# Second-layer operands moved to small buffers of their own, and the folded weights made in another buffer, in an attention-plus-FFN kernel

## The chip, the cores and the metric

The kernel runs on 1 core of a Trainium2 chip. The metric is the device time of one execution in microseconds (us). TensorE (PE) multiplies, VectorE (DVE) and ScalarE (ACT) do the elementwise work, SyncE (SP) issues the loads and GpSimd (POOL) the stores. Each engine works off its own list of instructions in order and waits on semaphores, so an instruction that waits holds up all that stands behind it in its list.

## The reference

For each of 4 batches (N = 6080 tokens, C = 256 channels) a channel attention, then a feed-forward network over all 24320 tokens:

```python
qn = q / (norm(q, axis=1) + 1e-06);  kn = k / (norm(k, axis=1) + 1e-06)
s = kn.transpose(0, 2, 1) @ qn / tau           # 256 x 256 for each batch
a = softmax(s)
x = (v @ a).reshape(24320, 256)
h = x @ w_in                                   # 256 -> 2048
return relu(h)**2 @ w_out                      # 2048 -> 256
```

## The kernel before

**The work.** The attention matrix of a batch is multiplied into w_in once (`fold7`), so that each token needs two products, 256 to 2048 and 2048 to 256. A float32 product is made as three of the shorter type fp32r: high by high, low by high, high by low; every operand therefore exists as a high part (an ACT or DVE cast) and a low part (a DVE subtraction). The first layer is a Winograd product of 2x2 blocks with 7 products instead of 8 (`m1` to `m7`, L600, three matmuls each), the second takes 8 units of three matmuls in each slot (`layer2`, L722).

**Chunks and slots.** The tokens run in 24 chunks, 6 for each batch; a chunk has T = 512 columns (the last of a batch 480) of two tokens each and 8 slots j of some 10 us, so a batch has 48 slots. In the slots j = 2 and 3 (`paired`, L581) the second layer of both slots together is a product of block pairs: `pair_unit` (L758, the operands K12 and KS4) and `pair_product` (L800, K11, KS2, KS3, K22, KS1), 42 matmuls instead of 48. Where T is below 512, each `pair_product` but K22's ends with a small matmul of 32 columns (L805) that closes the bank. The first and the last chunk are not paired.

**Operands.** First-layer operands of a slot (`wt`, 896 KB, 3 buffers) are loaded from the scratch `wsc` by `load_wt` (L527), second-layer operands (`wo`, 512 KB, 3 buffers) from `wosc` by `load_wo` (L182), those of the pair from `wss` by `load_ws` (L187), one or two at a time. They all go through SP's queue, in one order. Tile `th` (1 buffer) holds the split factors of the pair (`pair_split`, L786 and L787).

**Batch edges.** While a batch runs, the scores of the next are gathered; at slot 30 of the batch its attention matrix is made. Then, in slots 33 to 50, `fold7` makes the folded weights (PE L466, ACT L475 and L479), and `combine` (`combine_parts`, L500) turns them into first-layer operands: three casts on ACT (L518), three subtractions on DVE (L519) and a write to `wsc` from POOL (L521), one set in each of slots 40 to 43 and 47 to 50, built in a `wt` buffer. These stretches, some 100 us long, are called batch edges 1 to 3 here (about 500 to 650, 1040 to 1170 and 1560 to 1690 us).

**What sets the order.** The calls are written out by a table: `at(u, fn, ...)` puts a step at position u, counted in slots, and the engines' lists follow from that with a scheduler's choice in between. `TB`, `WB`, `OB` are numbers of buffers.

Of the kernel before, what the change touches and what calls it, by code (L numbers as in the profile page):

```python
# [16 lines left out]
P = 128  # L17
# [3 lines left out]
def tile_channel_attention_relu2_ffn(ctx, tc, kq, vT, tau, w_in, w_out, outT):  # L21
# [57 lines left out]
    SG = 1  # L79
    NP = 7  # L80
    K12, KS4, K11, KS2, KS3, K22, KS1 = range(NP)
    OB = 3
    wo = {}
    ws = {}
    wosc = {}
# [59 lines left out]
    def decode_w_out(g):  # L145
        W = work.tile([P, 4, C], F32, name="sq", tag="sq")
        decode_f64(raws.pop(("out", g)), W)
        halves = W.rearrange("p (f j) (e c) -> p j f e c", f=2, e=NH)
        for i in range(2):
            j = 2 * g + i  # L150
            w = wo[0, j] = work.tile([P, 2, 2, NH, P], F32R, name="wo", tag="wo", bufs=OB)
            nc.scalar.copy(out=w[:, 0], in_=halves[:, i])
            nc.vector.tensor_sub(out=w[:, 1], in0=halves[:, i], in1=w[:, 0])
            wosc[j] = scratch.tile([P, 2, 2, NH, P], F32, name=f"wosc{j}")
            nc.gpsimd.dma_start(out=wosc[j], in_=w.bitcast(F32))
            if g == SG:
                for k, f, e in ((K12, 1, 0), (K11, 0, 0), (K22, 1, 1)):
                    nc.gpsimd.dma_start(out=wss[:, k, i], in_=w[:, :, f, e].bitcast(F32))
        if g == SG:
            win["out"] = W  # L160

    def combine_w_out():

        W = win.pop("out").rearrange("p (f j) (e c) -> p f e j c", f=2, e=NH)
        a11, a12, a21, a22 = W[:, 0, 0], W[:, 1, 0], W[:, 0, 1], W[:, 1, 1]
        S = work.tile([P, 4, 2, P], F32, name="sq", tag="sq")
        s4, s2, s3, s1 = (S[:, i] for i in range(4))
        nc.vector.tensor_add(out=s1, in0=a21, in1=a22)
        nc.vector.tensor_sub(out=s2, in0=s1, in1=a11)
        nc.vector.tensor_sub(out=s3, in0=a11, in1=a21)  # L170
        nc.vector.tensor_sub(out=s4, in0=a12, in1=s2)
        for i, ks in enumerate(((KS4, KS2), (KS3, KS1))):
            x = S[:, 2 * i:2 * i + 2]
            w = work.tile([P, 2, 2, 2, P], F32R, name="wo", tag="wo", bufs=OB)
            nc.scalar.copy(out=w[:, :, :, 0], in_=x)
            nc.vector.tensor_sub(out=w[:, :, :, 1], in0=x, in1=w[:, :, :, 0])
            for k, half in zip(ks, range(2)):
                nc.gpsimd.dma_start(out=wss[:, k], in_=w[:, half].bitcast(F32))

    def load_wo(ci, j):  # L180
        w = wo[ci, j] = work.tile([P, 2, 2, NH, P], F32R, name="wo", tag="wo", bufs=OB)
        nc.sync.dma_start(out=w.bitcast(F32), in_=wosc[j])  # L182

    def load_ws(ci, k):
        n = min(2, NP - k)
        w = work.tile([P, 2, 2, 2, P], F32R, name="wo", tag="wo", bufs=OB)
        nc.sync.dma_start(out=w[:, :n].bitcast(F32), in_=wss[:, k:k + n])  # L187
        for i in range(n):
            ws[ci, k + i] = w[:, i]

# [310 lines left out]
    def combine_parts(b, g):  # L501

        eng = nc.vector
        u = us.pop((b, g))
        S = work.tile([P, 4, GW], F32, name="sq", tag="sq")
        s2, s3, s1, s4 = (S[:, i] for i in range(4))
        eng.tensor_add(out=s1, in0=u[:, 0, 1], in1=u[:, 1, 1])
        eng.tensor_sub(out=s2, in0=s1, in1=u[:, 0, 0])
        eng.tensor_sub(out=s3, in0=u[:, 0, 0], in1=u[:, 0, 1])
        eng.tensor_sub(out=s4, in0=u[:, 1, 0], in1=s2)  # L510
        for i in range(2):
            j = 2 * g + i
            if i and b:
                yield
            w = work.tile([P, 2, NP, P], F32R, name="wt", bufs=WB)
            js = slice(i * P, (i + 1) * P)
            for o, x in ((w[:, :, 0:2], u[:, :, 0, js]), (w[:, :, 2:3], u[:, 1:2, 1, js]), (w[:, :, 3:7], S[:, :, js])):
                nc.scalar.copy(out=o[:, 0], in_=x)  # L518
                eng.tensor_sub(out=o[:, 1], in0=x, in1=o[:, 0])  # L519
            wsc[b, j] = scratch.tile([P, 2, NP, P], F32, name=f"wsc{j}", bufs=2)  # L520
            nc.gpsimd.dma_start(out=wsc[b, j], in_=w.bitcast(F32))  # L521
            if b == 0:
                wt[0, j] = w
# [55 lines left out]
    raw2 = {}  # L579

    def paired(q):  # L581
        return 0 < q[0] < len(chunks) - 1 and q[1] // 2 == SG

    marks = {"ACT": [], "DVE": []}
    LEAD = 0.9
# [112 lines left out]
    def layer2(q, c, e):  # L698
# [12 lines left out]
        w = T // 2  # L711
        if tail and (c, e) == ("11", 0):
            ends["sum"] = work.tile([P, HMAX], F32, name="tt", tag="tt", bufs=TB)
            nc.scalar.copy(out=ends["sum"][:, :w], in_=outs[1, 1][:, w:T])
        spans = [(o, 0, T, first, last or final and j == NJ - 2 and (c, e) == ("12", 1))]
        if tail and n and e:
            if c == "22":
# [190 lines left out]
    def at(u, fn, *args):  # L908
        side.setdefault(round(u, 3), []).append((fn, args))
# [25 lines left out]
    for b in range(1, B):  # L935
        u0 = (b - 1) * QB
        first, last = (NJ + 2 if b == 1 else 0), 30
        for i in range(NT // 2):
            u, k = u0 + first + i * (last - first) // (NT // 2), 2 * i
            if k % G == 0:  # L940
                at(u - 3.4, score_load, b, k // G)
            at(u - 0.8, score_norm, b, k)
            if b > 1 or k > LATE[-1]:
                at(u - 1.0, score_split, b, k)
                at(u - 0.5, score_split, b, k + 1)
                at(u + MID, score_burst, b, [k, k + 1])
        end = u0 + last
        at(end - 0.6, squares_split, b)
        at(end + MID, norms_wide, b)
        at(end + 1.6, lambda b=b: exps(b, s_acc[b]))  # L950
        at(end + 2 + MID, attnT, b)
        for g in range(0, NG, 2):
            u = end + 3 + 3.5 * g
            if b == 1:
                at(u - 3.5, load_wins2, g)
            for i in range(NP):
                at(u + i - (0.7 if b == 1 else 2.5), right7, b, g, i)
                at(u + i + MID, fold7, b, g, i)
            for i in range(2):
                at(u + NP + 2 * i, combine, b, g + i)  # L960
                at(u + NP + 2 * i + 1, combine, b, g + i)
    for n, (ci, j) in enumerate(quads):
        if ci:
            at(n - 1.5, load_wt, ci, j)
            if not paired((ci, j)):
                at(n - 0.3, load_wo, ci, j)
            elif j % 2 == 0:
                for k, u in ((K12, -0.3), (K11, 0.3), (KS3, 3.75), (KS1, 5.0)):
                    at(n + u, load_ws, ci, k)
                for u, fn in ((2.2, right3), (2.6, right1), (2.8, right2), (3.4, right4)):  # L970
                    at(n + u, fn, ci)
                for u, k in ((3.1, KS2), (3.9, KS3), (4.85, K22), (5.3, KS1)):
                    at(n + u, pair_split, ci, k)
                for u, k in ((2.6, K11), (3.6, KS2), (4.6, KS3), (5.13, K22), (5.6, KS1)):
                    at(n + u, pair_product, ci, k)
# [84 lines left out]
```

## Time and profile before

| | us |
|---|---|
| median of 3 runs | 2135.79 |
| the three runs | 2134.65, 2135.79, 2140.91 |
| profiled execution, its own time | 2138.98 |
| its span in the profile | 2137.1 |
| PE busy | 2126.3 (99%) |
| DVE busy | 1816.0 (85%) |
| ACT busy | 1456.2 (68%) |
| POOL busy | 90.3 (4%) |

PE is busy for all but 10.8 us of the span, and its granted clock is 1.00 in every stretch. A matmul's busy time includes a modelled end that overlaps with the next one, so what a matmul costs is read from start to start of the rows of a timeline.

### The profile page before, as it was taken

To read this page: it belongs to the slowest core of one execution; us is meant where nothing else is said; L and a number is where in the kernel's file an instruction comes from. 1 tells how busy PE (TensorE), PEld (TensorE's weight loads), DVE (VectorE), ACT (ScalarE), POOL (GpSimd) and SP (SyncE) were. 2 spreads that over 40 slices of the span, in tenths; PEclk is the share of its full clock that TensorE was granted. 3 is DMA by queue.
4 is the path that set the end of the run, shared out by engine and by line. 5 is a ranking of instruction groups with operands and counts; after the bars stand their busy time and mean duration, and the time that the engine had idled before them with its cause. 6 is when DMAs were issued, how large, how long until landed. Compare 5 with 4: busy or idle time off the path is not lost.

```text
span 2137.1 us, 27056 instructions
## 1 busy us (share of the span) xinstructions
PE 2126.3 (99%) x9756; PEld 1775.4 (83%) x9756; DVE 1816.0 (85%) x2549; ACT 1456.2 (68%) x2411; POOL 90.3 (4%) x167
## 2 busy tenths in 40 slices
PE   9999999999999999999999999999999999999999
PEld 8888888888888888888888888888888888888888
DVE  7898999989999889898899988989789778778765
ACT  6787777766776767666667676767666656656654
POOL 0120000011000000000000000000000000000000
PEclk9999999999999999999999999999999999999999
DMA  9777755467785564456768555456576655555542
GB/s 362 296 285 271 248 188 193 165 245 256 254 309 202 187 227 158 174 195 219 270 222 303 204 189 207 156 176 224 198 269 225 233 180 185 177 180 182 179 170 83
DMA packets 101557, 461.83 MB, mean 216 GB/s; under 512 B 11824, under 2 KB 14512, under 8 KB 94640
## 3 DMA queue, kind: packets, MB, share of 16 engines
q1 hardware_dynamic: 85152, 391.23, 52.7%
q0 software_dynamic: 16128, 68.76, 8.1%
q8 instruction: 77, 1.26, 0.2%
q14 instruction: 56, 0.46, 0.1%
q10 hardware_dynamic: 144, 0.12, 0.0%
HBM read 390.33 MB, written 69.73 MB: 215 GB/s over the span
## 4 chain that ended last, share of the span: by engine, by line
issue 49%; PE 47%; POOL 2%; DMA 1%; ACT 1%; DVE 1%; POOLq 0%; ACTq 0%; SPq 0%
PE o L722 18%; PE h L600 11%; PE z L600 6%; PE x L600 3%; PE x L800 2%; PE x L240 2%; PE o L758 1%; POOL outT L743 1%; PE h L240 1%; PE o L240 1%; DMA wsc<-wt 1%; PE o L800 1%; PE h L420 0%; DMA kqt<-kq 0%; POOL wsc L521 0%
## 5 line engine op out<-in xcount | busy, mean ns | idle before, releaser
L722 PE MATMUL o<-g,wo 128*128 128x512 f32 (+1 forms) x3552 | 903.5, 388 | 0.7 <-DMA wo<-wosc 0.7
L722 PEld LDWEIGHTS o<-g,wo 128*128 128x128 f32 x3552 | 664.5, 188 | 135.4 <-DVE g L631 1.8
L600 PE MATMUL h<-vt,wt 128*128 128x512 f32 (+1 forms) x2304 | 616.3, 388 | 2.0 <-DMA wt<-wsc 1.6
L600 PEld LDWEIGHTS h<-vt,wt 128*128 128x128 f32 x2304 | 431.4, 188 | 93.0 <-ACT x L642 2.7
L600 PE MATMUL z<-vt,wt 128*128 128x512 f32 (+1 forms) x1152 | 325.4, 390 | 1.7 <-ACT z L651 1.4
L600 PEld LDWEIGHTS z<-vt,wt 128*128 128x128 f32 x1152 | 210.4, 188 | 45.0 <-ACT z L651 4.6
L620 DVE TENSOR_TENSOR g<-r,g 128x512 fp32r<-128x512 f32 (+1 forms) x296 | 201.7, 682 | 48.9 <-ACT g L619 46.7
L630 ACT CAST g<-s 128x1024 fp32r<-128x1024 f32 (+1 forms) x148 | 153.9, 1040 | 114.9 <-DVE s L629 114.7
L631 DVE TENSOR_TENSOR g<-s,g 128x1024 fp32r<-128x1024 f32 (+1 forms) x148 | 179.2, 1211 | 51.5 <-ACT g L630 50.6
L615 ACT ACTIVATE r<-z 128x512 f32<-128x512 f32 (+1 forms) x148 | 87.7, 592 | 176.2 <-PE z L600 168.7
L616 ACT ACTIVATE r<-r 128x512 f32<-128x512 f32 (+1 forms) x296 | 186.4, 630 | 5.8
L629 DVE SCALAR_TENSOR_TENSOR s<-s 128x1024 f32<-128x1024 f32 (+1 forms) x148 | 178.9, 1209 | 1.0
L600 PE MATMUL x<-vt,wt 128*128 128x512 f32 (+1 forms) x576 | 161.0, 387 | 0.0
L786 ACT CAST th<-pair 128x1024 fp32r<-128x1024 f32 (+1 forms) x88 | 92.1, 1046 | 91.8 <-PE x L800 77.2
L651 ACT COPY z<-h 128x512 f32<-128x512 f32 (+1 forms) x192 | 110.5, 575 | 33.8 <-PE h L600 33.6
L220 DVE TENSOR_TENSOR acc<-acc,sq 128x1024 f32<-128x1024 f32 x92 | 112.5, 1223 | 22.9 <-ACT sq L219 20.6
L600 PEld LDWEIGHTS x<-vt,wt 128*128 128x128 f32 x576 | 108.1, 188 | 21.6
L642 ACT COPY x<-h 128x512 f32<-128x512 f32 (+1 forms) x192 | 110.9, 578 | 4.1 <-PE h L600 3.7
L664 ACT COPY m<-h 128x512 f32<-128x512 f32 (+1 forms) x192 | 110.9, 578 | 1.0
L787 DVE TENSOR_TENSOR th<-pair,th 128x1024 fp32r<-128x1024 f32 (+1 forms) x88 | 106.5, 1210 | 1.9 <-ACT th L786 1.7
L572 DVE TENSOR_TENSOR vt<-v,vt 128x512 fp32r<-128x512 f32 (+1 forms) x144 | 95.9, 680 | 13.3 <-ACT vt L571 13.0
L669 DVE TENSOR_TENSOR s<-z,m 128x512 f32<-128x512 f32 (+1 forms) x148 | 100.6, 680 | 5.6 <-PE z L600 5.3
(201 smaller groups left out, 2673.9 us busy)
## 6 DMA issues: line engine op xcount, KB each, us to landing
wt<-wsc SPq DMA_DIRECT2D x184, 896.0 KB, 4.9
wo<-wosc SPq DMA_DIRECT2D x140, 512.0 KB, 3.7
kqt<-kq SPq DMA_DIRECT2D x47, 1024.0 KB, 7.4
wo<-wss SPq DMA_DIRECT2D x66, 512.0 KB, 5.3
wsc<-wt POOLq DMA_DIRECT2D x32, 896.0 KB, 6.1
v<-vT SPq DMA_DIRECT2D x40, 512.0 KB, 5.9
outT<-res POOLq DMA_DIRECT2D x80, 256.0 KB, 5.4
hl<-tsc SPq DMA_DIRECT2D x28, 512.0 KB, 3.7
```

The lines of the kernel that those rows point to most:

```text
L220: nc.vector.tensor_add(out=accs[b], in0=accs[b], in1=sq)
L600: nc.tensor.matmul(out=out[:, :T], lhsT=w[:, l, i], rhs=v[:, r, :T], start=start and n == 0, stop=n == 2, skip_group_check=True)
L616: nc.scalar.activation(out=r, in_=r, func=AF.Square)
L620: nc.vector.tensor_sub(out=hl[:, 1, :T], in0=r, in1=hl[:, 0, :T])
L629: nc.vector.scalar_tensor_tensor(out=s, in0=s, scalar=0.0, op0=ALU.max, in1=s, op1=ALU.mult)
L630: nc.scalar.copy(out=h, in_=s)
L631: nc.vector.tensor_sub(out=l, in0=s, in1=h)
L642: ins = nc.scalar.copy(out=st["X"][:, :T], in_=st["B"][:, :T])
L651: ins = nc.scalar.copy(out=st["Z"][:, :T], in_=st["B"][:, :T])
L664: nc.scalar.copy(out=state[q]["m7"][:, :T], in_=H[:, :T])
L722: nc.tensor.matmul(out=ps[:, lo:hi], lhsT=w2[:, l, f, e], rhs=r[:, lo:hi], start=start and k == 0, stop=stop and k == 2, skip_group_check= ...
L787: nc.vector.tensor_sub(out=l, in0=x, in1=h)
```

## The change

Five things are done. (1) `wo` has 2 buffers instead of 3; the memory set free holds two buffers of half the size, `ws`. The pair's operands K11, KS2, KS3, K22 and KS1 are loaded one by one into `ws` (`load_wss`, 256 KB each); only K12 and KS4 still share a `wo` buffer. The loads stand at other positions of the table. (2) At the start, `decode_w_out` and `combine_w_out` make the second-layer operands in a `pair` and a `th` tile instead of `wo` tiles, with fewer, wider instructions. (3) For the batches after the first, `combine` builds its set in the single buffer of `th` instead of in one of the three of `wt`; the first set of the later half stands 0.85 slots later. (4) The last chunk is paired too. (5) In the kernel's last slot, three results that ACT copied out are then sums with the pair's results, made by DVE (`layer2`, L739), and stored from SP's queue.

```diff
@@ -79,7 +79,7 @@
     SG = 1
     NP = 7
     K12, KS4, K11, KS2, KS3, K22, KS1 = range(NP)
-    OB = 3
+    OB = 2
     wo = {}
     ws = {}
     wosc = {}
@@ -145,17 +145,19 @@
     def decode_w_out(g):
         W = work.tile([P, 4, C], F32, name="sq", tag="sq")
         decode_f64(raws.pop(("out", g)), W)
-        halves = W.rearrange("p (f j) (e c) -> p j f e c", f=2, e=NH)
+        w = work.tile([P, 2, 2, 2, NH, P], F32R, name="pair", tag="pair", bufs=2)
+        halves = W.rearrange("p (f j) c -> p j f c", f=2)
+        h, l = (w[:, :, i].rearrange("p j f e c -> p j f (e c)") for i in range(2))
+        nc.scalar.copy(out=h, in_=halves)
+        nc.vector.tensor_sub(out=l, in0=halves, in1=h)
         for i in range(2):
             j = 2 * g + i
-            w = wo[0, j] = work.tile([P, 2, 2, NH, P], F32R, name="wo", tag="wo", bufs=OB)
-            nc.scalar.copy(out=w[:, 0], in_=halves[:, i])
-            nc.vector.tensor_sub(out=w[:, 1], in0=halves[:, i], in1=w[:, 0])
+            wo[0, j] = w[:, i]
             wosc[j] = scratch.tile([P, 2, 2, NH, P], F32, name=f"wosc{j}")
-            nc.gpsimd.dma_start(out=wosc[j], in_=w.bitcast(F32))
+            nc.gpsimd.dma_start(out=wosc[j], in_=w[:, i].bitcast(F32))
             if g == SG:
                 for k, f, e in ((K12, 1, 0), (K11, 0, 0), (K22, 1, 1)):
-                    nc.gpsimd.dma_start(out=wss[:, k, i], in_=w[:, :, f, e].bitcast(F32))
+                    nc.gpsimd.dma_start(out=wss[:, k, i], in_=w[:, i, :, f, e].bitcast(F32))
         if g == SG:
             win["out"] = W
 
@@ -169,22 +171,20 @@
         nc.vector.tensor_sub(out=s2, in0=s1, in1=a11)
         nc.vector.tensor_sub(out=s3, in0=a11, in1=a21)
         nc.vector.tensor_sub(out=s4, in0=a12, in1=s2)
-        for i, ks in enumerate(((KS4, KS2), (KS3, KS1))):
-            x = S[:, 2 * i:2 * i + 2]
-            w = work.tile([P, 2, 2, 2, P], F32R, name="wo", tag="wo", bufs=OB)
-            nc.scalar.copy(out=w[:, :, :, 0], in_=x)
-            nc.vector.tensor_sub(out=w[:, :, :, 1], in0=x, in1=w[:, :, :, 0])
-            for k, half in zip(ks, range(2)):
-                nc.gpsimd.dma_start(out=wss[:, k], in_=w[:, half].bitcast(F32))
+        w = work.tile([P, 4, 2, 2, P], F32R, name="th", tag="th", bufs=1)
+        nc.scalar.copy(out=w[:, :, :, 0], in_=S)
+        nc.vector.tensor_sub(out=w[:, :, :, 1], in0=S, in1=w[:, :, :, 0])
+        for i, k in enumerate((KS4, KS2, KS3, KS1)):
+            nc.gpsimd.dma_start(out=wss[:, k], in_=w[:, i].bitcast(F32))
 
     def load_wo(ci, j):
         w = wo[ci, j] = work.tile([P, 2, 2, NH, P], F32R, name="wo", tag="wo", bufs=OB)
         nc.sync.dma_start(out=w.bitcast(F32), in_=wosc[j])
 
-    def load_ws(ci, k):
-        n = min(2, NP - k)
-        w = work.tile([P, 2, 2, 2, P], F32R, name="wo", tag="wo", bufs=OB)
-        nc.sync.dma_start(out=w[:, :n].bitcast(F32), in_=wss[:, k:k + n])
+    def load_wss(ci, k, n=1):
+        tag, bufs = ("wo", OB) if n > 1 else ("ws", 2)
+        w = work.tile([P, n, 2, 2, P], F32R, name=tag, tag=tag, bufs=bufs)
+        nc.sync.dma_start(out=w.bitcast(F32), in_=wss[:, k:k + n])
         for i in range(n):
             ws[ci, k + i] = w[:, i]
 
@@ -512,7 +512,11 @@
             j = 2 * g + i
             if i and b:
                 yield
-            w = work.tile([P, 2, NP, P], F32R, name="wt", bufs=WB)
+            if b:
+                w = work.tile([P, 4 * HMAX], F32R, name="th", tag="th", bufs=1)
+                w = w[:, :2 * NP * P].rearrange("p (l i c) -> p l i c", l=2, i=NP)
+            else:
+                w = work.tile([P, 2, NP, P], F32R, name="wt", bufs=WB)
             js = slice(i * P, (i + 1) * P)
             for o, x in ((w[:, :, 0:2], u[:, :, 0, js]), (w[:, :, 2:3], u[:, 1:2, 1, js]), (w[:, :, 3:7], S[:, :, js])):
                 nc.scalar.copy(out=o[:, 0], in_=x)
@@ -579,7 +583,7 @@
     raw2 = {}
 
     def paired(q):
-        return 0 < q[0] < len(chunks) - 1 and q[1] // 2 == SG
+        return q[0] > 0 and q[1] // 2 == SG
 
     marks = {"ACT": [], "DVE": []}
     LEAD = 0.9
@@ -711,7 +715,7 @@
         w = T // 2
         if tail and (c, e) == ("11", 0):
             ends["sum"] = work.tile([P, HMAX], F32, name="tt", tag="tt", bufs=TB)
-            nc.scalar.copy(out=ends["sum"][:, :w], in_=outs[1, 1][:, w:T])
+            nc.vector.tensor_add(out=ends["sum"][:, :w], in0=sums2[ci, 1, 1][:, w:T], in1=outs[1, 1][:, w:T])
         spans = [(o, 0, T, first, last or final and j == NJ - 2 and (c, e) == ("12", 1))]
         if tail and n and e:
             if c == "22":
@@ -957,16 +961,16 @@
                 at(u + i - (0.7 if b == 1 else 2.5), right7, b, g, i)
                 at(u + i + MID, fold7, b, g, i)
             for i in range(2):
-                at(u + NP + 2 * i, combine, b, g + i)
+                at(u + NP + 2 * i + (0.85 if g and not i else 0), combine, b, g + i)
                 at(u + NP + 2 * i + 1, combine, b, g + i)
     for n, (ci, j) in enumerate(quads):
         if ci:
             at(n - 1.5, load_wt, ci, j)
             if not paired((ci, j)):
-                at(n - 0.3, load_wo, ci, j)
+                at(n + {4: 0.27, 5: -0.12}.get(j, -0.02), load_wo, ci, j)
             elif j % 2 == 0:
-                for k, u in ((K12, -0.3), (K11, 0.3), (KS3, 3.75), (KS1, 5.0)):
-                    at(n + u, load_ws, ci, k)
+                for u, *args in ((0.27, K12, 2), (-0.4, K11), (-0.3, KS2), (2.77, KS3), (3.77, K22), (4.77, KS1)):
+                    at(n + u, load_wss, ci, *args)
                 for u, fn in ((2.2, right3), (2.6, right1), (2.8, right2), (3.4, right4)):
                     at(n + u, fn, ci)
                 for u, k in ((3.1, KS2), (3.9, KS3), (4.85, K22), (5.3, KS1)):
```

Two places show how the lists of the engines move. In the names, `wt`, `wo`, `ws` and `th` are the tiles above, and the semaphores in brackets are those waited for: DMAHW of loads, DMASW of POOL's stores, the others of engines. Lines of the kernel after stand 4 further on than before from L516 on.

SP's list before, at the end of batch 1 (the rows from the load of a score tile `kqt` on):

```order
L202 DMA kqt<-kq 128x2048 [waits DMAHW5_49,DVE_49]
L527 DMA wt<-wsc_916 128x1792 [waits DMAHW6_49,DMAHW2_49,PE_49]
L182 DMA wo<-wosc_999 128x1024 [waits DMAHW7_49,PE_49]
L527 DMA wt<-wsc_1147 128x1792 [waits DMASW5_49,DMASW7_49,DMASW1_49,DVE_49]
L182 DMA wo<-wosc_1004 128x1024 [waits DMAHW1_49,PE_49]
L527 DMA wt<-wsc_1156 128x1792 [waits DMAHW4_49,PE_49]
```

SP's list after, at the same place:

```order
L202 DMA kqt<-kq 128x2048 [waits DMAHW7_49,DVE_49]
L531 DMA wt<-wsc_1135 128x1792 [waits DMAHW2_49,PE_49]
L182 DMA wo<-wosc_990 128x1024 [waits DMAHW3_49,PE_49]
L187 DMA ws<-wss 128x512 [waits PE_49]
L182 DMA wo<-wosc_992 128x1024 [waits DMAHW5_49,PE_49]
L531 DMA wt<-wsc_1144 128x1792 [waits DMAHW4_49,PE_49]
```

The load of `wt` that waits for POOL's stores (DMASW), with a load of `wo` behind it, waits for PE alone after the change.

ACT's list before, at the end of batch 2, in the slot in which `fold7`'s L479 stands (g is the operand of the second layer, x, m and z are copies of the first layer's sums):

```order
L479 COPY kqt<-h 128x512 [waits PE_49]
L615 ACTIVATE pair<-z 128x480 [waits PE_49]
L630 CAST g_9630<-pair 128x2x480 [waits DVE_49]
L642 COPY x<-h 128x480 [waits PE_49]
L664 COPY m_9664<-h 128x480 [waits PE_49]
L616 ACTIVATE pair<-pair 128x480 [waits Activation_49]
L518 CAST wt<-kqt 128x256 [waits DMASW2_49]
L518 CAST wt<-kqt 128x128
L651 COPY z<-h 128x480 [waits PE_49]
L518 CAST wt<-sq 128x512
```

ACT's list after, at the same place:

```order
L479 COPY kqt<-h 128x512 [waits PE_49]
L522 CAST th<-kqt 128x256 [waits DMASW2_49,DVE_49]
L522 CAST th<-kqt 128x128
L522 CAST th<-sq 128x512
L619 ACTIVATE pair<-z 128x480 [waits PE_49]
L634 CAST g_9657<-pair 128x2x480 [waits DVE_49]
L646 COPY x<-h 128x480 [waits PE_49]
```

DVE's list before, at the same place (the sums z and h of the first layer, their square, the low part of g, then the set's splits):

```order
L669 TENSOR_TENSOR pair<-z,m_9582 128x480 [waits PE_49]
L669 TENSOR_TENSOR pair<-h,m_9582 128x480 [waits PE_49]
L629 SCALAR_TENSOR_TENSOR pair<-pair 128x2x480 [waits DVE_49]
L631 TENSOR_TENSOR g_9630<-pair,g_9630 128x2x480 [waits Activation_49]
L519 TENSOR_TENSOR wt<-kqt,wt 128x256 [waits DMASW2_49,Activation_49]
```

DVE's list after, at the same place:

```order
L673 TENSOR_TENSOR pair<-z,m_9609 128x480 [waits PE_49]
L523 TENSOR_TENSOR th<-kqt,th 128x256 [waits DMASW2_49,Activation_49]
L673 TENSOR_TENSOR pair<-h,m_9609 128x480 [waits PE_49]
L523 TENSOR_TENSOR th<-kqt,th 128x128 [waits Activation_49]
L633 SCALAR_TENSOR_TENSOR pair<-pair 128x2x480 [waits DVE_49]
L523 TENSOR_TENSOR th<-sq,th 128x512 [waits Activation_49]
L635 TENSOR_TENSOR g_9657<-pair,g_9657 128x2x480 [waits Activation_49]
```

The casts of the set stand earlier than before, ahead of the activation of z, and still wait for a store (DMASW), now that of the set just before; the subtractions on DVE stand between the sums of the first layer.

## Rows read from the trace of the kernel before

**Rows 1.** Windows: us, busy us (x instructions) of PE, PEld, DVE, ACT, POOL; PEclk, DMA share, GB/s.

```profile
100.00:155.00 55.00, 54.81 (x239) 44.35 (x239) 53.49 (x83) 45.83 (x80) 13.01 (x22) 1.00 0.70 255
...
500.00:650.00 150.00, 147.49 (x688) 123.93 (x688) 138.00 (x213) 106.52 (x191) 12.25 (x22) 1.00 0.77 274
650.00:1040.00 390.00, 390.00 (x1830) 325.91 (x1829) 342.94 (x474) 266.22 (x435) 8.69 (x16) 1.00 0.56 195
1040.00:1170.00 130.00, 128.20 (x601) 108.56 (x600) 114.36 (x175) 90.82 (x163) 8.83 (x16) 1.00 0.78 282
```

**Rows 2.** The page's part 5, PE: busy us, mean ns, idle before and its releaser.

```profile
L722 PE MATMUL o<-g,wo 128*128 128x512 f32 (+1 forms) x3552 | 903.5, 388 | 0.7 <-DMA wo<-wosc 0.7
...
L600 PE MATMUL h<-vt,wt 128*128 128x512 f32 (+1 forms) x2304 | 616.3, 388 | 2.0 <-DMA wt<-wsc 1.6
...
L600 PE MATMUL z<-vt,wt 128*128 128x512 f32 (+1 forms) x1152 | 325.4, 390 | 1.7 <-ACT z L651 1.4
```

**Rows 3.** Timeline of PE, edge 1: start us, us, engine line op [idle before <-releaser].

```profile
553.67 0.81 PE L600 MATMUL z<-vt,wt 128*128 128x480 f32 x3
555.10 1.54 PE L600 MATMUL h<-vt,wt 128*128 128x480 f32 x6 [0.62 <-DMA wt<-wsc]
...
557.34 1.57 PE L722 MATMUL o<-g,wo 128*128 128x480 f32 x6 [0.69 <-DMA wo<-wosc]
```

**Rows 4.** Waits of SP's queue, 540 to 560: us in total, times, longest.

```profile
SPq L527 <- DMA wsc<-wt: 6.3, 1, 6.3
```

**Rows 5.** Timeline of PE, then ACT, at the end of batch 2.

```profile
1069.97 0.86 PE L466 MATMUL h<-hl,aT 128*128 128x512 f32 x3
1072.28 0.91 PE L600 MATMUL z<-vt,wt 128*128 128x480 f32 x3 [1.44 <-ACT z L651]
...
1071.16 0.60 ACT L518 CAST wt<-kqt 128x256 fp32r<-128x256 f32 x2 [2.42 <-DMA wsc<-wt]
```

**Rows 6.** Landing of the stores to wsc (L521): of all 32; of that at 1063.1.

```profile
DMA to landing us min/median/max: 3.8/6.1/11.7
...
DMA to landing us min/median/max: 8.0/8.0/8.0
```

**Rows 7.** Timelines of DVE, POOL, ACT and PE around the sets of edge 2.

```profile
1048.15 0.68 DVE L735 TENSOR_TENSOR res<-res,o 128x512 f32<-128x512 f32 x1
...
1050.71 0.68 DVE L519 TENSOR_TENSOR wt<-sq,wt 128x512 fp32r<-128x512 f32 x1
...
1051.69 0.54 POOL L521 DMA_DIRECT2D wsc<-wt  x1 [2.02 <-DVE wt L519]
...
1064.30 0.65 DVE L669 TENSOR_TENSOR pair<-h,m 128x480 f32<-128x480 f32 x1
1064.98 1.16 DVE L629 SCALAR_TENSOR_TENSOR pair<-pair 128x960 f32<-128x960 f32 x1
...
1067.18 0.56 ACT L642 COPY x<-h 128x480 f32<-128x480 f32 x1
...
1059.08 0.81 PE L600 MATMUL h<-vt,wt 128*128 128x480 f32 x3
...
1068.24 0.81 PE L600 MATMUL h<-vt,wt 128*128 128x480 f32 x3
```

**Rows 8.** Timeline of PE in a paired chunk of 480 columns.

```profile
1081.82 1.46 PE L800 MATMUL x<-g,wo 128*128 128x480 f32 x6
1083.12 0.18 PE L805 MATMUL x<-ones_r 128*128 128x32 f32 x1
1083.15 1.12 PE L758 MATMUL o<-g,wo 128*128 128x480 f32 x4
1084.11 0.81 PE L600 MATMUL z<-vt,wt 128*128 128x480 f32 x3
```

**Rows 9.** Timeline of DVE at the end of the span.

```profile
2133.46 0.41 DVE L737 TENSOR_TENSOR tt<-tt,h 128x240 f32<-128x240 f32 x1 [1.99 <-PE h L722]
```

**Rows 10.** Landing of the transfers of tile wo, over the whole span.

```profile
DMA to landing us min/median/max: 2.7/4.2/13.3
```

## The prediction

> **What bounds the kernel now.** I read the share of each engine first, then the stretches, then who PE waited for, then the waits of SP's queue and of ACT at those places, and last the landings of transfers. PE is the bound: in the steady stretch it is busy for 390.00 of 390.00 us at a granted clock of 1.00, while ACT and DVE have room [rows 1]. What it loses, it loses at the batch edges: 150.00 - 147.49 = 2.51 us at edge 1 and 130.00 - 128.20 = 1.80 us at edge 2; the DMA share is 0.77 and 0.78 there, against 0.56 between [rows 1]. The first stretch shown, where operands are still being made, loses 0.19 us. So the change can win in two ways only: fewer matmuls, and these few microseconds of idle time. That alone sets how large a gain can be.
>
> The releasers name two kinds of loss [rows 2]. L722 and L600 (h) wait 0.7 + 1.6 = 2.3 us for loads of wo and wt; L600 (z) waits 1.4 us for ACT's copy of z. Recorded idle time understates the cost, because a start after a wait is followed by a slow one. At the first place [rows 3] three matmuls of 480 columns go before 555.10, and six before 557.34. Six such cost 1.30 us from 1081.82 to 1083.12 [rows 8], so 0.217 each. The loss is (1.43 - 0.65) + (2.24 - 1.30) = 1.72 us where 0.62 + 0.69 = 1.31 us is recorded: 1.31 times as much.
>
> **Loads at the batch edges: -3.0 us.** Why do these loads come late? SP's queue waited 6.3 us, once, at the load of wt (L527) for a store to wsc from wt [rows 4]. That is the row of SP's list before that waits for DMASW: the buffer it loads into was last filled by `combine` and is free only when POOL's store has been read out of it. The load of wo behind it, whose buffer may be free long before, waits too; this is the 0.69 us of L722. The change builds the sets in th, so that every load of wt waits only for PE, and the loads stand in the order in which buffers come free. If that holds, the 2.3 us at these waits go, times 1.31 = 3.0 us. What is late next is the landing itself, with the DMA engines at 0.77. Bounds: all stays (0) or all goes (-3.0). I take -3.0, since the row names the store and the store leaves this queue.
>
> **Sets at the batch edges: -1.6 and +3.6 us.** First the gain. At the end of batch 2 ACT's cast of a set waited 2.42 us for a store, the copy of z stands behind that cast on ACT, and PE's next product started 2.31 us after the fold's three matmuls at 1069.97 [rows 5]. Three matmuls of 512 columns cost 0.217 x 3 x 512/480 = 0.69 us, so 1.62 us was lost. The cast stands elsewhere after the change, and this loss goes: -1.6.
>
> Now the price. th has one buffer, so that each set's first cast waits until the store of the set before it has landed, where wt gave three buffers in turn. Behind the cast on ACT stand the activation of z, the cast of g and the copy of x; behind the split on DVE the sum of h and the square (L633). PE waits for the copy of x. For the sets of slots 42 and 43 at edge 2 I work this out from [rows 7] and a landing L.
> Set 42 waits for the store of set 41. That store left at 1051.69, 0.30 us after its last split (1050.71 + 0.68). After the change this split stands behind the addition that ended at 1048.83 and two smaller splits (by width 0.34 + 0.17 us), so it ends about 1050.0 and the store leaves at 1050.3. It lands at 1050.3 + L; a cast and a split of about 0.4 us each, then the square starts, and 2.76 us later (from 1064.98 to the end of the copy at 1067.74) x is there. PE wants it at 1059.08. With L = 6.1, the median of all 32 stores [rows 6]: 1056.4 + 0.8 + 2.76 = 1059.96, so 0.9 us late.
> Set 43 waits for the store of set 42. That leaves after the square (1057.2 + 1.16), two splits (0.85) and 0.3: 1059.5. It lands at 1065.6; with 0.8 for cast and split, another split of 0.2 and the 3.44 us from the sum of h (1064.30) to the end of the copy of x, x is there at 1070.0. PE wants it at 1068.24, and 0.9 later by the first delay: 0.9 us late again. Sum 1.8 us for an edge.
> By the quickest landing, 3.8 us [rows 6], set 42 has x at 1057.7 and set 43 before 1068.24 too: nothing. By 8.0 us, the landing of the store at 1063.1 [rows 6], it is 2.8 + 2.8 = 5.6 us for an edge.
> Edge 3 is laid out as edge 2, and I count both: 2 x 1.8 = +3.6 (bounds 0 and 11.2). I take the median because the DMA engines are busier here than elsewhere [rows 1], which speaks against the quickest. Edge 1 has the casts of the sets at other places, mostly behind the g cast, where one buffer costs what three did: 0, and at worst as much as edge 2. The sets of slots 47.85 to 50 have no fold beside them, and set 41 follows a store in a quieter time: 0.
>
> The Trainium skill ("DMA: Bandwidth & Descriptors", section "Anatomy of one DMA — SWDGE (gpsimd) path") gives a store from GpSimd about 2.0 us fixed, mostly until the write is confirmed, plus its bytes over 436 KB per us. For 896 KB that is an estimate of 4.1 us; the quickest store here, 3.8 us, agrees, the median of 6.1 us does not. By that rule the sets would cost nothing, which is rival 1 below.
>
> **The last chunk: -0.8 us.** 42 instead of 48 matmuls of 480 columns: -6 x 0.217 = -1.30. Four small matmuls come in. From 1083.12 to 1084.11 one of them and four others took 0.99 us [rows 8], 4 x 0.217 = 0.87 without it: 0.12 each, +0.48. Sum -0.82. The work of the pair (splits, sums) lies on ACT and DVE, with room. In the last slot copies become DVE sums; DVE idles 1.99 us ahead of its last sum [rows 9], so 0, and 0.41 (one such sum) if it had no room.
>
> **Start and steady state: 0.** The wider casts and splits of the operands save some instructions beside PE, which loses only 0.19 us from 100 to 155 [rows 1]: a gain is at most 0.2. Loads of wo and ws now stand ahead of others there and wait for stores; the nearest price for a load that comes late is the 0.94 us before 557.34 [rows 3]. I take 0. In the steady state PE has no idle time to win. The 256 KB loads are more in number and equal in bytes; two wo buffers leave, by the table, 0.86 of a slot from release to use. A slot of 480 columns is 1068.24 - 1059.08 = 9.16 us [rows 7], so 7.9 us, against a median landing of 4.2 [rows 10]: 0.
>
> **Sum.** -3.0 - 1.6 + 3.6 - 0.8 = -1.8 us. Made against the profiled execution of 2138.98 us this is 2137.2 us; that execution lies 3.19 us above the median of the runs, 2135.79, so the forecast is 2134.0 us. 0.3% of the median, 6.4 us, is about what a measurement of this kernel can tell from no change.
>
> **Rivals.**
> (1) Every store to wsc lands in about 4 us, since the loads around it are spread better. Then the sets cost nothing: -3.0 - 1.6 - 0.8 = -5.4, 2130.4 us. For it: the quickest are at 3.8. Against: half of the 32 took over 6.1 us.
> (2) The loads stay late, because the batch edge is short of DMA time and not of buffers: two wo buffers and a landing of up to 13.3 us [rows 10] against a window of 7.9. The change doesn't do what it says, the -3.0 stays away, the sets' price remains: +1.2, 2137.0 us. For it: the DMA share at the edges. Against: SP's 6.3 us stood at a semaphore, not at a landing of its own.
> (3) Slower: the single th buffer becomes the bound at all three edges, with stores landing at 8.0 us: 3 x 5.6 - 5.4 = +11.4, 2147.2 us. It decides from new stalls of 5.4 + 6.4 = 11.8 us, 3.9 an edge, which is a landing of about 7.2 us. For it: the store at 1063.1 took 8.0 and the slowest 11.7. Against: the median, and that edge 1 is laid out otherwise.
>
> **How the numbers follow.** Forecast 0.47, rival 1 0.25, rival 2 0.17, rival 3 0.07, and 0.04 for something not looked at, half to either side. From rival 1's 2130.4 less the start's 0.2 and the 1.1 us between two of the runs, 2129.0 is the low end; edges 2 and 3 at 8.0 us give -5.4 + 11.2 = +5.8, 2141.6, the high end. Faster by over 0.3% means below 2129.4, 1.0 us past rival 1: a quarter of it and 0.02, so 0.08. Slower means above 2142.2: rival 3 and 0.02, so 0.09. The rest, 0.83, is the same.
>
> **What would show it.** In the profile after: no wait of SP's L531 for a store to wsc, and no idle time of PE for wt or wo at the edges (loads right); waits of ACT's L522 for DMA wsc<-th at edges 2 and 3 with idle time of PE's L604 behind a copy of x, of 1 to 3 us an edge (sets right; none: rival 1); 9754 matmuls, of which PE's busy time falls by about 1 us (last chunk). I am wrong if PE's idle time at the edges stays for loads (rival 2), grows past 4 us an edge for the sets (rival 3), or turns up in the steady stretches, which I put at 0.

## The result and the profile after

The changed kernel is slower: 2156.66 us in the median of 5 runs (2154.44 to 2159.14) against 2136.76 us for the kernel before in 5 runs, ratio 1.0092, 95% interval 1.0076 to 1.0107. The forecast was 2134.0 us, with 2141.6 as its upper end. The profiled execution has a span of 2154.7 us against 2137.1, so 17.6 us have to be found.

The stretches come first, in two halves for each batch edge: the first has the sets of slots 40 to 43, the later one those of 47.85 to 50. Columns as in [rows 1]. Before:

```profile
500.00:570.00 70.00, 68.17 (x308) 56.89 (x308) 62.68 (x100) 44.78 (x85) 7.92 (x14) 1.00 0.80 279
570.00:650.00 80.00, 79.32 (x382) 67.05 (x381) 75.33 (x114) 61.73 (x108) 4.33 (x8) 1.00 0.74 270
1040.00:1100.00 60.00, 58.54 (x267) 49.43 (x266) 49.48 (x75) 37.70 (x70) 4.32 (x8) 1.00 0.84 305
1100.00:1170.00 70.00, 69.66 (x335) 59.13 (x335) 64.88 (x101) 53.12 (x94) 4.51 (x8) 1.00 0.73 261
1560.00:1630.00 70.00, 69.90 (x318) 58.98 (x317) 59.81 (x94) 44.06 (x81) 4.32 (x8) 1.00 0.75 272
1630.00:1700.00 70.00, 70.00 (x316) 58.58 (x315) 60.04 (x91) 46.55 (x84) 4.33 (x8) 1.00 0.65 230
```

After:

```profile
500.00:570.00 70.00, 68.19 (x310) 57.22 (x309) 62.52 (x100) 45.58 (x85) 6.98 (x13) 1.00 0.82 288
570.00:650.00 80.00, 77.07 (x365) 64.27 (x364) 71.98 (x110) 59.34 (x103) 4.32 (x8) 1.00 0.72 260
1040.00:1100.00 60.00, 57.43 (x261) 48.36 (x260) 48.04 (x76) 35.96 (x66) 4.31 (x8) 1.00 0.81 295
1100.00:1170.00 70.00, 65.31 (x302) 54.65 (x302) 57.22 (x89) 48.45 (x85) 4.49 (x8) 0.95 0.69 248
1560.00:1630.00 70.00, 68.06 (x302) 57.48 (x301) 56.31 (x88) 45.38 (x83) 4.32 (x8) 0.98 0.78 267
1630.00:1700.00 70.00, 66.62 (x292) 55.18 (x291) 54.23 (x85) 43.07 (x76) 4.32 (x8) 0.98 0.61 216
```

PE's idle time in the first halves is 1.83 + 1.46 + 0.10 = 3.4 us before and 1.81 + 2.57 + 1.94 = 6.3 us after: 2.9 more. In the later halves it is 0.68 + 0.34 + 0 = 1.0 before and 2.93 + 4.69 + 3.38 = 11.0 after: 10.0 more, in stretches for which I had written 0. The granted clock is below 1.00 in three of the six, which it was nowhere before. Between the edges nothing moved: 390.00 of 390.00 us from 650 to 1040 as before.

PE's waits of the kernel after, against [rows 2] (us in total, times, longest):

```profile
PE h L604 <- ACT x L646: 8.1, 7, 1.9
PE z L604 <- DVE s L673: 6.6, 3, 3.2
PE o L726 <- DMA wo<-wosc: 1.5, 1, 1.5
```

PE no longer waits for loads of wt. It waits for the copy of x on ACT and for the first layer's sums on DVE. And what holds ACT? Its one large wait for a transfer, 500 to 1700 us:

```profile
ACT th L522 <- DMA wsc<-th: 38.0, 12, 4.8
```

The landing of the 24 stores from th and 8 from wt has also grown, against [rows 6]:

```profile
DMA to landing us min/median/max: 3.8/6.7/11.4
```

How such a wait reaches PE, at the later half of edge 2 (timelines of ACT, DVE and PE):

```profile
1131.05 0.62 ACT L225 CAST hl<-kqt 128x512 fp32r<-128x512 f32 x1
1136.37 0.61 ACT L522 CAST th<-kqt 128x256 fp32r<-128x256 f32 x2 [4.70 <-DMA wsc<-th]
...
1138.84 0.58 ACT L646 COPY x<-h 128x512 f32<-128x512 f32 x1
...
1146.61 0.60 ACT L522 CAST th<-kqt 128x256 fp32r<-128x256 f32 x2 [3.00 <-DMA wsc<-th]
...
1147.05 0.63 DVE L523 TENSOR_TENSOR th<-kqt,th 128x256 fp32r<-128x256 f32 x2 [3.28 <-ACT th L522]
...
1149.13 0.68 DVE L673 TENSOR_TENSOR s<-z,m 128x512 f32<-128x512 f32 x1
...
1139.48 0.96 PE L604 MATMUL h<-vt,wt 128*128 128x512 f32 x3 [1.49 <-ACT x L646]
...
1149.87 1.65 PE L604 MATMUL z<-vt,wt 128*128 128x512 f32 x3 [3.20 <-DVE s L673]
1151.31 2.76 PE L604 MATMUL h<-vt,wt 128*128 128x512 f32 x6
1153.87 2.41 PE L726 MATMUL o<-g,wo 128*128 128x512 f32 x6
1156.12 0.86 PE L604 MATMUL h<-vt,wt 128*128 128x512 f32 x3
```

The first cast waits 4.70 us for the store of the set before, and the copy of x behind it makes PE wait 1.49. One slot later the cast waits 3.00, DVE's split waits for the cast, the sum L673 stands behind the split in DVE's list, and PE waits 3.20. Then six matmuls of 512 columns take 2.56 us from 1151.31 to 1153.87 instead of 1.40 (those from 1135.05 to 1136.45): the granted clock had fallen, as the window shows:

```profile
1150.00:1156.00 6.00, 6.00 (x15) 4.70 (x16) 4.81 (x7) 3.66 (x6) 0.00 (x0) 0.52 0.87 306
1156.00:1166.00 10.00, 10.00 (x52) 8.47 (x51) 7.47 (x12) 5.46 (x12) 0.54 (x1) 1.00 0.80 272
```

Summed from start to start over the slowed matmuls, the clock cost about 2.8 us here, 1.6 us at 1599 and 1.5 us at 1685.

The whole account is read from start to start: the same matmul is looked up in the timelines of both kernels (at the end of edge 2 one starts at 1170.10 us before and at 1180.00 after).

| stretch | after less before, us |
|---|---|
| start, to 500 | -1.7 |
| first halves of edges 1, 2 and 3 | -0.4, +1.3, +3.1 |
| later halves of edges 1, 2 and 3 | +3.0, +7.6, +5.7 |
| between the edges | 0.0 |
| from 2030 to the end | -1.1 |

The edges lose 20.4 us, 16.4 of them in the later halves. Of the 20.4, 12.9 are idle time and 5.9 the clock; the remaining 1.6 lie in what recorded idle time leaves out at a wait (at 1061.49, for instance, 1.30 us are recorded, 1.46 are lost from start to start, and the product behind it takes 0.10 longer). The -1.7 at the start is not a gain of the change: 1.39 us of it is a wait for kqt at 53.42 in the profiled execution of the kernel before, which the executions of e6 and e9, with the same start, do not have. Against e9 the kernel after reaches 500 us within 0.1 us.

### The profile page after: what moved, and what is told of

Its sections match the earlier page's. It is cut to its first block, busy times and chain, and to the rows that moved or that the text cites. A ratio compares the mean times of both kernels' runs of the same rounds, so it can differ in the third digit from the quotient of the medians.

```text
span 2154.7 us, 27105 instructions
## 1 busy us (share of the span) xinstructions
PE 2132.2 (99%) x9754; PEld 1778.2 (83%) x9754; DVE 1826.2 (85%) x2558; ACT 1460.3 (68%) x2405; POOL 89.9 (4%) x167
## 4 chain that ended last, share of the span: by engine, by line
issue 47%; PE 47%; POOL 2%; DMA 2%; ACT 1%; DVE 1%; POOLq 0%; ACTq 0%
PE o L726 17%; PE h L604 11%; PE z L604 6%; PE x L604 3%; PE x L804 3%; PE x L240 2%; PE o L762 1%; POOL outT L747 1%; DMA wsc<-th 1%; PE o L240 1%; PE h L240 1%; PE o L804 1%; DMA wo<-wosc 0%; PE h L420 0%; PE h L466 0%
## 5 line engine op out<-in xcount | busy, mean ns | idle before, releaser
L726 PE MATMUL o<-g,wo 128*128 128x512 f32 (+1 forms) x3312 | 844.5, 389 | 1.5 <-DMA wo<-wosc 1.5
L726 PEld LDWEIGHTS o<-g,wo 128*128 128x128 f32 x3312 | 621.6, 188 | 127.8 <-DMA wo<-wosc 1.9
L790 ACT CAST th<-pair 128x1024 fp32r<-128x1024 f32 (+1 forms) x92 | 96.0, 1043 | 97.9 <-PE x L804 77.4
L604 PEld LDWEIGHTS x<-vt,wt 128*128 128x128 f32 x576 | 108.5, 188 | 21.9
L791 DVE TENSOR_TENSOR th<-pair,th 128x1024 fp32r<-128x1024 f32 (+1 forms) x92 | 111.0, 1207 | 4.2 <-ACT th L790 4.1
L804 PE MATMUL x<-th,ws 128*128 128x512 f32 (+1 forms) x414 | 106.1, 389 | 0.0
```

The costliest lines, as they stand in the source:

```text
L604: nc.tensor.matmul(out=out[:, :T], lhsT=w[:, l, i], rhs=v[:, r, :T], start=start and n == 0, stop=n == 2, skip_group_check=True)
L726: nc.tensor.matmul(out=ps[:, lo:hi], lhsT=w2[:, l, f, e], rhs=r[:, lo:hi], start=start and k == 0, stop=stop and k == 2, skip_group_check= ...
L791: nc.vector.tensor_sub(out=l, in0=x, in1=h)
L804: nc.tensor.matmul(out=ps[:, :T], lhsT=w[:, l], rhs=r, start=k != K22 and i + n == 0, stop=k != K22 and i == 1 and n == 2, skip_group_chec ...
```

## The experiments

Two causes stood against each other at first: the chain of stores through the single th buffer (theory A), and the loads of the change, with two wo buffers and a new order of SP's queue (theory B). From e5 on there is a third, the shift of the later half's first set by 0.85 slots (theory C).

**e1: sets in wt again.** The edit, in the changed kernel:

```diff
-            if b:
-                w = work.tile([P, 4 * HMAX], F32R, name="th", tag="th", bufs=1)
-                w = w[:, :2 * NP * P].rearrange("p (l i c) -> p l i c", l=2, i=NP)
-            else:
-                w = work.tile([P, 2, NP, P], F32R, name="wt", bufs=WB)
+            w = work.tile([P, 2, NP, P], F32R, name="wt", bufs=WB)
```

> The changed kernel with one thing undone: combine builds its sets in the three wt buffers again; the loads, the last chunk and the start stay as changed. Theory A (the chain of stores through the single th buffer made the loss: ACT waited 38.0 us for stores, 12 times, and PE idled 17.3 us at the three batch edges instead of 4.4): the time falls to 2131 to 2138 us, PE idles at most 5 us over the edges, and the granted clock is 1.00 throughout. Theory B (two wo buffers and many small loads made the loss, by longer landings and a new order of SP's queue): it stays above 2150 us.

Measured: 2149.95 us, ratio to the kernel before 1.0057 (1.0043 to 1.0070). Neither theory: some 7 us came back, 14 stayed. The idle time that stayed lies at 615, 1150 and 1682 us, all in later halves, with ACT waiting 21.9 us for stores from wt. The chain through th is one cause, not the only one.

**e2: the sets in th alone**, in the kernel before, with the shift of 0.85 slots (the reverse of e1's edit, and the line of e6).

> The kernel before with one part of the change alone: combine builds its sets in th, with the first set of the later half 0.85 slots later. Theory A: 2150 to 2160 us, with ACT's casts waiting 30 us or more for stores and PE idle some 17 us at the edges. Theory B: 2133 to 2138 us.

Measured: 2159.42 us, 1.0107 (1.0094 to 1.0121). These lines alone carry the whole loss; the rest of the change did not make it. Theory B falls.

**e3: every other set in th.**

```diff
-            if b:
+            if b and i == 0:
                 w = work.tile([P, 4 * HMAX], F32R, name="th", tag="th", bufs=1)
```

> The changed kernel, but only every other set (the first of each pair) is built in th, the second in a wt buffer. Each set in th then follows a store that left two sets earlier, some 20 us. Theory A: ACT's waits for stores go (below 5 us in all), 2131 to 2137 us; what is left are loads of wt behind every second store. Theory B: above 2150 us.

Measured: 2131.98 us, 0.9982 (0.9973 to 0.9991): faster than the kernel before. PE waits at the edges only for loads of wt (2.4 us), and ACT hardly waits for stores (500 to 1700 us: in total, times, longest):

```profile
ACT th L522 <- DMA wsc<-th: 2.7, 2, 1.7
```

**e4: each set stored twice.**

```diff
             nc.gpsimd.dma_start(out=wsc[b, j], in_=w.bitcast(F32))
+            if b:
+                again = scratch.tile([P, 2, NP, P], F32, name=f"again{j}", bufs=2)
+                nc.gpsimd.dma_start(out=again, in_=w.bitcast(F32))
```

> The changed kernel, where each set of the batches after the first is stored twice, the second time to a scratch that nobody reads, so that th comes free later by one more store of 896 KB (some 3 us or more by the landings of 3.8 to 11.4 us). Theory A: ACT's waits for stores grow by about 3 us at each of 18 sets, and PE's idle time with them, since no slack is left at most of them: 2175 to 2205 us. Theory B: at most 5 us more than the changed kernel, 2156 to 2162 us, for 21 MB more DMA work.

Measured: 2164.5 us, 1.0133 (1.0120 to 1.0147). It lies between the two ranges: 10 us and more below that of theory A, 2.5 above that of theory B. ACT's waits did not grow, they are 35.5 us in all. PE's idle time did grow, so there is more loss, but not as a fixed place of the casts would give. ACT's list offers a reason: with two stores the casts of the second, third and fourth set of edge 1 are its rows 597, 612 and 627, with one store they are rows 596, 604 and 622. So the order of the list follows what has to be stored. How much of the loss is the 21 MB of added transfers was not separated.

**e5 and e6: the shift.** e1 left the later halves. There one more line had changed. e5 takes it back in e1's kernel, e6 puts it alone into the kernel before:

```diff
-                at(u + NP + 2 * i, combine, b, g + i)
+                at(u + NP + 2 * i + (0.85 if g and not i else 0), combine, b, g + i)
                 at(u + NP + 2 * i + 1, combine, b, g + i)
```

> As e1 (sets in the wt buffers, the rest as changed), but the first set of the later half back at position 47 instead of 47.85. In e1 PE's idle time lies almost only behind the later half's sets, at 615, 1150 and 1682 us. Theory C (the shift by 0.85 puts the first set of the later half 0.15 slots ahead of the second, which then finds no buffer free and waits for a whole store): the later half's idle time goes, 2130 to 2135 us, granted clock 1.00 throughout. Theory B (the loads of the change, two wo buffers among them, disturb the later half): it stays at 2147 to 2152 us.

> The kernel before with the shift of 0.85 slots alone, sets in wt. Theory C: 2145 to 2152 us, with idle time of PE behind the sets of the later half of 2.5 us or more at each edge, and the granted clock at 0.50 behind the longest. Theory B: 2133 to 2138 us, as before.

Measured: e5 2135.39 us, 0.9991 (0.9982 to 1.0000); e6 2150.93 us, 1.0058 (1.0042 to 1.0073). The shift alone costs some 12 to 14 us, without any th. In e6 the first two sets of the later half are stored at 594.85 and 601.61 us, where the kernel before stored them at 585.46 and 597.56. The second store of e6 leaves behind loads of kqt, wt and wo on SP at 597.54, 600.58 and 601.23. It lands after 10.2 us, where the kernel before took 4.4 (the second stores at edges 2 and 3: 9.6 and 9.4 against 4.3 and 3.9):

```profile
DMA to landing us min/median/max: 10.2/10.2/10.2
```

and the next set's cast waits for it (timelines of ACT, DVE and PE of e6):

```profile
611.86 0.60 ACT L518 CAST wt<-kqt 128x256 fp32r<-128x256 f32 x2 [6.06 <-DMA wsc<-wt]
...
612.29 0.63 DVE L519 TENSOR_TENSOR wt<-kqt,wt 128x256 fp32r<-128x256 f32 x2 [5.37 <-ACT wt L518]
...
614.22 0.68 DVE L669 TENSOR_TENSOR s<-z,m 128x512 f32<-128x512 f32 x1
...
614.96 1.65 PE L600 MATMUL z<-vt,wt 128*128 128x512 f32 x3 [4.09 <-DVE s L669]
```

**e7: the shift taken back, the sets left in th.**

> The changed kernel with the first set of the later half back at 47; the sets stay in the single th buffer. Theory C with the chain of stores: the later half's idle time goes (some 2.7, 5.0 and 3.7 us and the clock behind it), what is left is the first half's, 1.7, 3.0 and 2.1 us by the changed kernel's own trace: 2138 to 2146 us; more where the first set of the later half now meets the pair's last split in th. If the chain of stores alone is the cause, whatever the position: 2152 to 2160 us.

Measured: 2142.44 us, 1.0022 (1.0013 to 1.0032). The later halves lose nothing:

```profile
570.00:650.00 80.00, 80.00 (x386) 67.63 (x386) 76.00 (x114) 62.63 (x110) 4.31 (x8) 1.00 0.76 267
1100.00:1170.00 70.00, 70.00 (x338) 59.29 (x337) 64.63 (x101) 54.13 (x97) 4.32 (x8) 1.00 0.75 269
1630.00:1700.00 70.00, 70.00 (x314) 57.91 (x313) 58.72 (x91) 47.51 (x85) 4.31 (x8) 1.00 0.67 234
```

The first halves still lose 3.2, 3.5 and 1.7 us of idle time. With e1, e5 and the changed kernel this makes a square on the same loads, as ratios to the kernel before:

| | no shift | shift |
|---|---|---|
| sets in wt | 0.9991 (e5) | 1.0057 (e1) |
| sets in th | 1.0022 (e7) | 1.0092 (changed kernel) |

The shift costs 0.0066 and 0.0070, the single buffer 0.0031 and 0.0035: about 14 and 7 us, and they add up. This holds where all sets of the batches after the first go through one kind of buffer; with both kinds in turn it is otherwise (e3 and e11, below).

**e8: the later half's sets further apart.** The positions 47.85, 49.0, 50.15, 51.3 in the changed kernel:

```diff
-                at(u + NP + 2 * i + (0.85 if g and not i else 0), combine, b, g + i)
-                at(u + NP + 2 * i + 1, combine, b, g + i)
+                at(u + NP + (2.3 * i + 0.85 if g else 2 * i), combine, b, g + i)
+                at(u + NP + (2.3 * i + 2 if g else 2 * i + 1), combine, b, g + i)
```

> The changed kernel with the later half's four sets at 47.85, 49.0, 50.15 and 51.3 instead of 47.85, 48, 49 and 50: the shift stays, the distance between sets in th becomes 1.15 slots. Theory C: as e7, 2138 to 2146 us. If the shift hurts by its place and not by the distance to the next set: 2150 us or more.

Measured: 2149.91 us, 1.0055 (1.0041 to 1.0068). Theory C, that the short distance of 0.15 slots does the harm, falls as I put it: with 1.15 slots ACT waits even longer for stores, 48.3 us in 14 waits, though 7 us of time came back. With th alone the later place costs time even so. It does not by itself: e3 has the same shift, its stores there took up to 9.9 us, and it is faster than the kernel before, because next to no cast waits for them. Which transfers make the stores slow I did not take apart further than e6's rows.

**e9: the last chunk alone** (the lines of `paired` and `ends["sum"]` in the kernel before).

> The kernel before with its last chunk paired too and the last results made by sums on DVE, nothing else. By the prediction's step: 6 matmuls of 480 columns less, 4 small ones more, -0.8 us, 2134 to 2137 us beside a kernel before of 2136; the rival is that the pair's splits and sums do not fit into the last slots and cost 1 us or more.

Measured: 2136.33 us against 2137.38, 0.9991 (0.9982 to 1.0001), which alone does not tell it from no change. The traces tell it more sharply: from the six products that begin at 2049.61 to the start of the last matmuls at 2132.92 it is 83.31 us before, and from 2048.12 to 2130.45 in e9, 82.33: -0.98 us, where the step said -0.82.

**e10 and e11: every other set in th, no shift.** e10 takes the second set of each pair (`if b and i == 1`), e11 the first, both at 47.

> The changed kernel without the shift of 0.85, and with only the second set of each pair built in th, the first in a wt buffer. By the two causes found (the shift, and stores through one th buffer) nothing of the loss is left: 2129 to 2134 us. If the pair's last split in th and the set at 48 collide, it is above 2136 us.

> As e3 (first set of each pair in th, second in wt), but without the shift of 0.85. If the shift has a use, it is here: at 47 the set in th meets the pair's last split in th. Then 2133 to 2142 us, with waits of ACT or DVE for a store ahead of the split of the pair; otherwise as e3, 2130 to 2134 us.

Measured: e10 2131.00 us, 0.9967 (0.9955 to 0.9978); e11 2131.35 us, 0.9971 (0.9960 to 0.9983). Both are faster than both kernels. Against e11, e3 has the shift besides: start to start it cost 1.4 us in their traces, where it cost some 14 with one kind of buffer. So the shift does its harm through casts that wait for a store. And e11 hints at what the shift was for: ACT's split of the pair (L790) waits 2.1 us for stores from th there, in two waits; in e10 no instruction of ACT waits for a store. e10's edges, to be read against the first table:

```profile
500.00:570.00 70.00, 69.58 (x318) 59.03 (x317) 65.16 (x103) 47.48 (x88) 7.00 (x13) 1.00 0.85 306
570.00:650.00 80.00, 80.00 (x388) 68.04 (x387) 75.77 (x115) 60.36 (x105) 4.33 (x8) 1.00 0.68 245
1040.00:1100.00 60.00, 60.00 (x278) 51.34 (x277) 50.46 (x76) 38.47 (x69) 2.58 (x5) 1.00 0.78 294
```

**e12: half of each store.**

```diff
-            nc.gpsimd.dma_start(out=wsc[b, j], in_=w.bitcast(F32))
+            if b:
+                nc.gpsimd.dma_start(out=wsc[b, j][:, 0], in_=w[:, 0].bitcast(F32))
+                nc.gpsimd.dma_start(out=wsc[b, j][:, 1], in_=wsc[b - 1, j][:, 1])
```

> The changed kernel, where of each set of the batches after the first only the high half (448 KB) is stored from th; the low half in wsc is copied from the batch before instead, DRAM to DRAM, behind it on POOL's queue (so the products use a wrong low half, and the time is read without regard to that). th comes free after half the bytes. If the loss is the landing against a fixed place of the casts, ACT's waits fall from 38.0 to below 20 us, PE's idle time with them, and the time is 2138 to 2148 us. If the order of ACT's list is made with the store's size in view, the casts stand earlier than in the changed kernel (the lists show it: the second and third set of edge 1 at rows 590 and 599 instead of 596 and 604) and the slack is as short as before: waits of 28 to 40 us and 2150 to 2160 us.

Measured: 2148.48 us, 1.0067 (1.0045 to 1.0090), 5 to 7 us less than the changed kernel, and in neither range; ACT waits 29.5 us in 11 waits, at the foot of the second range. Half the bytes took away less than a quarter of the waiting. Two things go with that, and this run does not separate them: the casts stand earlier in the list (rows 590 and 599), and the landing itself fell only from a median of 6.6 to 5.0 us. With e4 it shows that the places of the casts follow what has to be stored; that this keeps the slack short with one buffer is likely, but argued. With a second buffer in turn (e3, e10, e11) the waits are gone or small.

## Why the prediction was wrong, step by step

**What bounds the kernel: right, with a hole.** PE's idle time at the edges was all there was to win, and e10 won it but for 0.4 us, with the last chunk shorter besides. That its 2131.0 us is near the first rival's 2130.4 is no success of that rival: e10 is another kernel, and the stores of the changed kernel did not land in 4 us. But the same sentence has no floor below: an edge can lose far more than the 2.5 us that it lost before.

**Sets of the later half, "0": the step that failed.** I put them at 0 because no fold stands beside them, and passed over the shift of 0.85 as a mere place. It moved the first set to 0.15 slots ahead of the second, and made it some 10 us later (its store at edge 1 left at 585.43 us in e7 and at 595.14 in the changed kernel), to a place where the stores land late: the first two of each later half took 3.8 to 4.4 us before and 6.7 to 8.1 after. A cast one slot or less behind then waits for them (3.5, 4.7 and 3.8 us for the second set). That is 10.0 of 12.9 us of new idle time, and by e1 and e5 to e7 some 14 us with the clock. Without the shift the forecast would still have been too low, but inside its range: e7's ratio of 1.0022 makes 2140.5 us of 2135.79. The rival for "slower" named the single buffer at all three edges and needed 3.9 us an edge, at a landing of 7.2 us; the edges lost 2.2, 5.5 and 5.2 us more in idle time. Its mechanism, ACT's cast waiting for the store before it, is what the trace shows, but it was priced for the first halves and not for the later ones, where landings were 7.7 and 8.1 us at edge 2.

**Sets of the first half, +3.6: right in kind, too small.** Start to start, edge 2 lost 3.0 us at three places (1061, 1070 and 1072) and edge 3 2.1 at one, and 1.6 more there by the clock, where the step said 1.8 each. Edge 1 lost nothing there, as the step said. It goes on in the order that the step foresaw: store, cast, split, sum, copy of x, PE.

**Loads, -3.0: about half came.** No load of wt waits for a store from `combine` at the edges any more: SP's waits of 63.6 us in all for wsc<-wt have become 1.0. The idle time for wt went; start to start this gave back 0.95 us at 634 and 0.63 at 1163, 1.6 of 3.0. The first place, at 555, lost 1.7 us as before, with another cause:

```profile
555.25 1.57 PE L726 MATMUL o<-g,wo 128*128 128x480 f32 x6 [1.53 <-DMA wo<-wosc]
```

There the load of wo waits on SP behind loads whose buffers come free from PE, the longest wait being 4.7 us at a load of ws; its median landing rose from 3.7 to 5.1 us. That was rival 2, at one place of three.

**The copy of z, -1.6: went** at the place that [rows 5] show; its successor is the copy of x.

**Last chunk, -0.8: right**, -0.98 by e9.

**What no step had: the clock.** 5.9 of the edges' 20.4 us are slower matmuls behind idle time. I had read 1.00 in every row of before and treated an idle microsecond as one microsecond. The bound of "slower" should have stood wider for that alone.

**Start and steady state, 0: right.** From 100 to 155 us PE is busy 54.79 against 54.81, and 390.00 of 390.00 in the steady stretches. The wait of 1.39 us at 53.42 lay ahead of the stretch that [rows 1] show; it raised the execution from which the sum was made, not the kernel.

The Trainium skill's price of a store ("DMA: Bandwidth & Descriptors", section "Anatomy of one DMA — SWDGE (gpsimd) path"), an estimate of 4.1 us for 896 KB, held for the quickest (3.8) again and for few others: the median was 6.1 before and 6.7 after. Had I gone by it I would have been further off.

## What to carry to other kernels

A buffer with one instance that is filled on ACT and DVE and emptied by a store puts the store's landing into the lists of ACT and DVE; count everything that stands behind the fill there, and take the slow landings of that stretch, not the median of all. A shift of a fraction of a slot in a table of positions is a change of its own: look at the distance to its neighbours, at the transfers it then runs beside and at who waits for the buffer, and try it alone. Two kinds of buffers in turn gave both gains of this change and neither loss (e10), and made the shift nearly harmless (e3).

## What was not expected of the hardware

A stall of PE can cost more than its length. Behind some, the granted clock fell to the lower of its two levels (1.2 instead of 2.4 GHz) for a few microseconds: in the kernel after behind the stall of 3.20 us at 1149.87 (0.52 on average from 1150 to 1156, above), and behind this one, where six matmuls of 480 columns took 1.73 us instead of 1.30 (kernel after, PE):

```profile
1599.43 1.55 PE L604 MATMUL h<-vt,wt 128*128 128x480 f32 x3 [1.94 <-ACT x L646]
1600.77 1.40 PE L604 MATMUL x<-vt,wt 128*128 128x480 f32 x3
1601.97 1.89 PE L726 MATMUL o<-g,wo 128*128 128x480 f32 x6
1603.70 0.85 PE L466 MATMUL h<-hl,aT 128*128 128x512 f32 x3
```

But not behind a longer one, in e7, where the clock stays 1.00 (timeline, then the window behind it):

```profile
556.77 1.56 PE L726 MATMUL o<-g,wo 128*128 128x480 f32 x6 [2.85 <-DMA wo<-wosc]
...
556.00:564.00 8.00, 7.23 (x33) 6.26 (x34) 4.78 (x8) 3.29 (x6) 0.00 (x0) 1.00 0.25 104
```

At the same product of e2 a shorter stall, 2.61 us at 558.71, was followed by a mean clock of 0.57 up to 562, and the six matmuls took 2.21 us instead of 1.39. So the length of the stall alone does not decide it. One kernel differs from execution to execution as well: e7's ten runs reach from 2138.07 us at a mean granted clock of 1.000 to 2146.32 us at 0.997. What decides it was not tried.
